# Attention, expert layer and dense layer on one core: the second pair of remainders in four column groups, the dense layer ending with 448 rows, the read in two row tiles

## The chip, the core and the metric

The kernel runs as one launch on one core of a Trainium2 chip. The metric is device time in microseconds of that core. Before the change three runs took 575.08, 575.28 and 576.47 us; the median, 575.28, is the time to compare with.

## What is computed

```python
B, H, S, Ns, D = (4, 8, 512, 32, 64)          # attention
N, D, E, F = (2304, 512, 8, 1024)             # expert layer
n_tokens, d_model, d_ff = (2304, 512, 2048)   # dense layer
...
a = softmax(scale * x @ state.T)              # 512 x 32 per head
xread = a @ state
a2 = softmax(scale * state @ x.T)             # 32 x 512 per head
sread = a2 @ x
rows = concat([xread, sread])                 # 4 * 544 = 2176 rows of 512
...
logits = rows @ w_gate
expert = argmax(logits); gate = softmax(logits)[expert]
disp[e, n] = the n-th row of expert e, while n < capacity
y = relu(disp @ w1[e]) @ w2[e]                # 512 -> 1024 -> 512
out = gate * y[expert, place]                 # zero for rows over capacity
...
h = out @ w_in                                # 512 -> 2048
result = (h * clip(h + 3, 0, 6) / 6) @ w_out  # 2048 -> 512
```

The capacity is 576 rows for each of the 8 experts. In this text layer one is the expert layer and layer two the dense layer.

## The kernel before

**Attention** (`phase1`) goes over the four batches. A batch has eight heads, in two halves f of four heads. `soft_max`, `turn`, `read_max`, `read_exp`, `read_sum` and `read_turn` make the read weights `aT`, 128 partitions (four heads of 32 states) by 128 rows. `read` (line 335) then computes, for block j of 128 rows and half f, one fp32 matmul with K = 128: the stationary operand is `aT`, the moving one is `bd`, a block-diagonal matrix of 264 columns, four heads of 64 values and 8 columns that give the gate's logits. There are 8 reads for each batch, 32 in all; each goes to a PSUM tile `psX` (pool `pX`, three buffers) and is copied to `xrow` by ScalarE (line 344) or, where the table `ALT` says so, by VectorE (line 342). `rows_out` adds the logits of the two halves (line 348) and writes rows of 536 floats to `x_rows` in DRAM.

The order of the instructions of this phase comes from a scheduler: `ln` gives the main steps their order, the tables `AFTER` and `AHEAD` hang side steps to them (`count`, `place`, `lists`, which turn logits into lists of rows by expert, and all of the first expert's tile, named `e_...` and `w..`). `tables` (line 649) then makes small tables on VectorE: `tab` with the expert and rows of each full tile, `tabh` with those of each remainder, `trips` for the loop at the end.

**Layer one.** Up to 256 rows of an expert make a full tile; an expert's remainder of 1 to 64 rows is a half. Six full tiles (NF = 6) and four halves (NQ = 4) are computed in straight code, what is beyond that in a loop at the end. A full tile (`m1`, `m2`) splits weights and rows in two fp32r parts and sums three products. The halves go two by two as a pair (PAIRS: pair 0 beside tile 2, pair 1 beside tile 4), in fp32, the 64 rows of an expert being 64 columns of the array and each expert its own column group:

```python
T.matmul(ps[n][64 * g:64 * g + 64, :],
         th[:, 128 * k + 64 * g:128 * k + 64 * g + 64],
         raws[k, g][:, 512 * n:512 * n + 512], ...)
```

That is line 1070 in `p_m1`. `p_ht` transposes its result (line 1082), `p_m2` (line 1090) is the second layer, `p_y` transposes and writes 128 rows to `y_pad` (line 1099). From here on the order is the order of the code, engine by engine.

**Layer two** works on column tiles of 256 rows: tiles 0 to 5 are the full tiles, tile 6 holds the two pairs. For each of 16 slices m of the 2048 hidden values, `mm3` (line 1115) does twelve fp32r matmuls with 256 moving columns (three products by four blocks of 128), ScalarE and VectorE make the activation and split it in `gh` and `gl` (lines 1127 to 1130), and `mm4` (line 1138) does, for each block t of 128 rows, three matmuls with 512 moving columns into PSUM. `mm4` of a slice is issued behind `mm3` of the next one. Tiles 0 and 1 make the first group, beside which the weights of the layer are converted from 64-bit inputs (`vload`, `vconv`, `prep`); tiles 2 to 6 follow one at a time. `put` (line 1256) scales a block of the result and writes it with an indirect DMA on POOL's queue. In the last tile the second block's `mm4` of the last seven slices (NH) is held back, so that the first block's write is done beside it.

## Time and profile before

| what | value |
|---|---|
| median of three runs | 575.28 us |
| the profiled execution | 573.73 us |
| its span, first to last instruction | 571.5 us |
| PE busy | 550.7 us, 96% |
| DVE busy | 309.8 us, 54% |
| ACT busy | 222.2 us, 39% |
| POOL busy | 142.5 us, 25% |
| mean granted clock of PE | 0.995 |

PE is TensorE, DVE VectorE, ACT ScalarE, POOL GpSimd. The profiled execution took 2.2 us more than its span, which is what lies around the first and the last instruction. A busy engine is not one at its peak: a matmul's record reaches past the start of the next one. An fp32 matmul has two records in the trace, an fp32r matmul one. The attention runs to about 105 us of the span, layer one to 251, the first group of layer two to 343, the last two tiles from 478 to the end.

### The profile page before, as it was taken

What the parts mean: (1) busy time and instruction counts of PE and PEld (TensorE: products, weight loads), DVE (VectorE), ACT (ScalarE), POOL (GpSimd) and SP (SyncE); (2) the same over time, 40 slices, a digit from 0 to 9 for tenths busy, and PEclk for the clock granted to TensorE, in tenths of its full rate; (3) what the DMA queues carried; (4) which work ended last, traced back from release to release, by engine and by line L of the source; (5) the groups of instructions that cost most, each with busy time, mean ns of one, the idle gap of its engine ahead of it and who ended that gap; (6) DMA issues with size and microseconds to landing.
All of it is one profiled execution on the core that took longest, in us unless ns stands there. A gap on an engine that the chain in (4) does not pass through costs nothing.

```text
span 571.5 us, 10466 instructions
## 1 busy us (share of the span) xinstructions
PE 550.7 (96%) x3954; PEld 478.8 (84%) x3954; DVE 309.8 (54%) x700; ACT 222.2 (39%) x462; POOL 142.5 (25%) x195
## 2 busy tenths in 40 slices
PE   6999789999999999999999999999999999999996
PEld 3665589887969696999999889999999999999994
DVE  4888985439625674567778953343333234234331
ACT  4878632235114150424434353333333333333331
POOL 5335734212400110017767732001001001001001
PEclk9999899999999999999999999999999999999999
DMA  6836621997979794235754311001001001000000
GB/s 136 181 122 208 231 103 52 333 377 246 353 260 395 253 342 149 79 124 191 254 204 124 134 39 75 0 24 53 1 18 57 1 18 57 1 1 19 19 2 30
DMA packets 52201, 75.26 MB, mean 132 GB/s; under 512 B 23121, under 2 KB 31313, under 8 KB 51634
## 3 DMA queue, kind: packets, MB, share of 16 engines
q1 hardware_dynamic: 49634, 67.09, 34.9%
q0 software_dynamic: 2240, 7.38, 3.8%
q8 instruction: 33, 0.54, 0.4%
q14 instruction: 22, 0.18, 0.1%
q10 hardware_dynamic: 272, 0.07, 0.1%
HBM read 70.75 MB, written 16.49 MB: 153 GB/s over the span
## 4 chain that ended last, share of the span: by engine, by line
issue 37%; PE 28%; DMA 9%; DVE 5%; ACT 1%; POOL 0%; POOLq 0%; DVEq 0%; ACTq 0%
PE pm L809 10%; PE pm L798 9%; DMA out_dram<-o,fid 6%; PE pm L1090 2%; PE pm L1070 2%; DMA st<-in_moe_w_out_dram 2%; PE p L1115 2%; DVE v L943 2%; DMA st<-in_moe_w_in_dram 1%; DVE v L939 1%; DVE g L1128 1%; DVE v L941 1%; PE po L1138 1%; ACT wh L957 1%; PE pxt L764 1%
## 5 line engine op out<-in xcount | busy, mean ns | idle before, releaser
L1115 PE MATMUL p<-yTh,wh 128*128 128x256 f32 x448 | 110.5, 280 | 0.0
L1115 PE MATMUL p<-yTl,wh 128*128 128x256 f32 x448 | 110.5, 280 | 0.0
L1128 DVE SCALAR_TENSOR_TENSOR g<-u,p 128x256 f32<-128x256 f32 x110 | 46.1, 419 | 115.9 <-ACT u L1127 115.8
L1127 ACT ACTIVATE u<-p,b 128x256 f32<-128x256 f32 x110 | 52.1, 474 | 109.1 <-PE p L1115 109.1
L1115 PEld LDWEIGHTS p<-yTl,wh 128*128 128x128 f32 x448 | 84.4, 188 | 3.9
L1115 PEld LDWEIGHTS p<-yTh,wh 128*128 128x128 f32 x448 | 84.4, 188 | 3.8
L1138 PE MATMUL po<-wh,gh 128*128 128x512 f32 x220 | 86.3, 392 | 0.0
L1138 PE MATMUL po<-wh,gl 128*128 128x512 f32 x220 | 86.2, 392 | 0.0
L1138 PE MATMUL po<-wl,gh 128*128 128x512 f32 x220 | 86.1, 391 | 0.0
L1129 ACT CAST gh<-g 128x256 fp32r<-128x256 f32 x110 | 44.7, 406 | 80.0 <-DVE g L1128 80.0
L1115 PE MATMUL p<-yTh,wl 128*128 128x256 f32 x448 | 71.5, 282 | 0.9 <-POOL wl L958 0.9
L1262 POOL DMA_INDIRECT out_dram<-o,fid x14 | 13.7, 977 | 219.7 <-ACT o L1261 163.6
L1115 PEld LDWEIGHTS p<-yTh,wl 128*128 128x128 f32 x448 | 60.8, 189 | 1.5 <-POOL wl L958 1.5
L1130 DVE TENSOR_TENSOR gl<-g,gh 128x256 fp32r<-128x256 f32 x84 | 36.8, 438 | 39.8 <-ACT gh L1129 39.8
L1138 PEld LDWEIGHTS po<-wh,gl 128*128 128x128 f32 x220 | 41.2, 187 | 9.7 <-POOL gl L1130 0.4
L1138 PEld LDWEIGHTS po<-wh,gh 128*128 128x128 f32 x220 | 41.4, 188 | 5.3
L1138 PEld LDWEIGHTS po<-wl,gh 128*128 128x128 f32 x220 | 41.4, 188 | 5.2
L809 PE MATMUL pm<-hth,w2h 128*128 128x256 f32 x160 | 45.5, 284 | 0.0
L798 PE MATMUL pm<-xth,w1h 128*128 128x256 f32 x160 | 44.6, 283 | 0.7 <-ACT xth L758 0.7
L809 PE MATMUL pm<-hth,w2l 128*128 128x256 f32 x160 | 45.1, 282 | 0.0
L809 PE MATMUL pm<-htl,w2h 128*128 128x256 f32 x160 | 45.0, 282 | 0.0
L958 POOL TENSOR_TENSOR wl<-v,wh 128x1024 fp32r<-128x1024 f32 x14 | 34.8, 2489 | 40.3 <-DMA st<-in_moe_w_in_dram 38.2
(285 smaller groups left out, 1005.1 us busy)
## 6 DMA issues: line engine op xcount, KB each, us to landing
raw<-in_moe_w_dram SPq DMA_DIRECT2D x80, 512.0 KB
st<-in_moe_w_in_dram SPq DMA_DIRECT2D x16, 512.0 KB
st<-in_moe_w_out_dram SPq DMA_DIRECT2D x16, 512.0 KB
x_rows<-xrow SPq DMA_DIRECT2D x4, 1072.0 KB
xb<-in_x_dram SPq DMA_DIRECT2D x32, 128.0 KB
yg<-y_pad SPq DMA_DIRECT2D x14, 258.0 KB
out_dram<-zt SPq DMA_DIRECT2D x2, 1536.0 KB
y_pad<-y SPq DMA_DIRECT2D x5, 516.0 KB
```

The source lines that it names most:

```text
L798: T.matmul(ps[:, j], W1[l][k][:, ls], xT[r][:, k], start=n == 0, stop=n == 11)
L809: T.matmul(ps[:, j], W2[l][k // 2][:, k % 2, ls], hT[k // 2][r][:, k % 2], start=k == 0 and i == 0, stop=k == 7 and i == 2)
L943: V.scalar_tensor_tensor(out=t, in0=lo, scalar=29, in1=t, op0=ALU.logical_shift_right, op1=ALU.bitwise_or)
L958: (V if m in (0, 2) else G).tensor_tensor(out=wl, in0=v, in1=wh.bitcast(F32), op=ALU.subtract)
L1070: T.matmul(ps[n][64 * g:64 * g + 64, :], th[:, 128 * k + 64 * g:128 * k + 64 * g + 64], raws[k, g][:, 512 * n:512 * n + 512], start=i == 0 ...
L1115: T.matmul(pv, l[:, 128 * k:128 * k + 128], r[:, :, 128 * k:128 * k + 128], start=n == 0, stop=n == 11)
L1127: A.activation(out=u, in_=ps, func=AF.Relu, bias=b3)
L1128: V.scalar_tensor_tensor(out=g, in0=u, scalar=6.0, in1=ps, op0=ALU.min, op1=ALU.mult)
L1129: A.copy(gh, g)
L1130: eng.tensor_tensor(out=gl, in0=g, in1=gh.bitcast(F32), op=ALU.subtract)
L1138: T.matmul(po[t], l[:, ls], r[:, 512:1024], start=m == 0 and i == 0, stop=m == 15 and i == 2)
L1262: G.indirect_dma_start(out=out, out_offset=bass.IndirectOffsetOnAxis(ap=fid[:, t:t + 1], axis=0), in_=o, in_offset=None, bounds_check=B * ...
```

## The change

**Layer two** ends with one group of 448 rows in place of the tiles 5 and 6: the 256 rows of tile 5, the 128 of pair 0 and 64 of pair 1. `mm3_j` does the twelve matmuls with 448 moving columns and `act3` twice, for 256 and for 192 columns. `mm4_j` does three matmuls for each of three blocks and two for the last: its 64 rows of `gl` stand beside its 64 rows of `gh` in one stationary operand, and `put(..., half=True)` adds the two halves of the sum. The sums of the last two blocks for the slices after HJ = 12 are held back to the end. **Pair 1** is now for experts whose remainder is at most 32 rows (`halves` sorts the remainders and gives the places): 32 columns of the array for each expert and half of the 1024 hidden values, so four column groups, and in its second layer four groups of 256 moving columns in place of two of 512. **The read** is done with 64 array rows at a time: `bd` has 136 columns (two heads and the logits), and a group of four matmuls fills two PSUM tiles of two blocks each; rows of `x_rows` have 548 floats. `halves` takes over what `tables` did for the remainders, and the copies for the loop (`listed`) are issued later.

```diff
-        ps = pX.tile([128, 264], F32, name="psX", tag="X")
-        T.matmul(ps, s["aT"][:, f, j, :], bd[:, 2 * b + f, :], start=True, stop=True)
...
+        u, a = divmod(i, 2)
+        j0, f = 2 * (u // 2), u % 2
+        if a == 0:
+            s["px"] = [pX.tile([128, 2, 136], F32, name="psX", tag="X") for _ in range(2)]
+            for j in range(2):
+                for r in range(2):
+                    T.matmul(s["px"][r][:, j], s["aT"][64 * r:64 * r + 64, f, j0 + j, :], bd[64 * r:64 * r + 64, 2 * b + f, :], start=True, stop=True)
+        g = PW * (2 * f + a)
+        (V.tensor_copy if f"rd{b}{i}" in ALT else A.copy)(s["xrow"][:, j0:j0 + 2, g:g + 136], s["px"][a])
...
-    for i in (0, 2, 4, 6, 1, 3, 5, 7):
+    for i in range(8):
         ln(read, B - 1, i)
...
-NQ, NHM = 4, 8
+NQ, NHM = 4, 10
...
+NJ = 448
+HJ = 12
...
+    def halves():
+        c, f, te = cnt, Q[0][:, 0, 4:12], Q[3][:, 0, 4:12]
+        q, h = Q[0][:, 1, 4:12], Q[0][:, 2, 4:12]
+        V.tensor_scalar(out=c32, in0=c, scalar1=-32.0, scalar2=None, op0=ALU.add)
+        V.scalar_tensor_tensor(out=q, in0=f, scalar=256.0, in1=c32, op0=ALU.mult, op1=ALU.is_lt)
+        V.scalar_tensor_tensor(out=h, in0=f, scalar=256.0, in1=c, op0=ALU.mult, op1=ALU.is_lt)
...
+    def p_rows(p, g):
+        return [(64 * g, 64)] if p == 0 else [(32 * g, 32), (64 + 32 * g, 32)]
...
-    def p_m1(th, raws):
+    def p_m1(p, th, raws):
+        nb = 2 - p
...
+                    s, w = p_rows(p, g)[n if p else 0]
+                    T.matmul(ps[0 if p else n][s:s + w, :], th[:, 128 * k + s:128 * k + s + w], raws[k, g][:, 512 * n:512 * n + 512],
...
+            for n in range(1 + p):
+                for g in range(2):
+                    if p:
+                        s, m, a = 64 * n + 32 * g, 32, 128 * (k % 4) + 64 * (k // 4) + 32 * g
+                    T.matmul(ps[s:s + m, :], th[:, a:a + m], raws[k // 2, g][:, 512 * (k % 2) + 256 * n:512 * (k % 2) + 256 * n + w],
...
+        if w == 192:
+            gl, tail = gl[:, 0:128], gh[:, 192:256]
+            V.tensor_tensor(out=tail, in0=g[:, 128:192], in1=gh[:, 128:192].bitcast(F32), op=ALU.subtract)
...
+    def mm3_j(m, yTh, yTl):
+        ps = bank3(NJ)
+        sums3(m, ps, *(lambda k, v=v: v[:, k] for v in (yTh, yTl)))
+        return act3(ps[:, 0:256], 256), act3(ps[:, 256:NJ], NJ - 256)
...
+    def mm4_j(m, gg, po, ts):
+        wh, wl = (w[:, 512:1024] for w in WM[m])
+        for t in ts:
+            gh, gl = gg[t // 2]
+            ls = slice(128 * (t % 2), 128 * (t % 2) + 128)
+            ops = ((gh, wh), (gh, wl), (gl, wh)) if t < 3 else ((gh, wh), (gh, wl))
+            for i, (l, r) in enumerate(ops):
+                T.matmul(po[t], l[:, ls], r, start=m == 0 and i == 0, stop=m == 15 and i + 1 == len(ops))
...
-    groups = [(0, 1)] + [(c,) for c in range(2, NCS)]
+    groups = [(0, 1)] + [(c,) for c in range(2, NCS - 2)]
...
+    for m in range(16):
+        gj[m] = mm3_j(m, jh, jl)
+        if m == 0:
+            finish(late)
+            pj = [pM.tile([128, 512], F32, name="po", tag="M") for t in range(4)]
+        else:
+            mm4_j(m - 1, gj[m - 1], pj, (0, 1) if m > HJ else (0, 1, 2, 3))
+    mm4_j(HJ, gj[HJ], pj, (2, 3))
+    for t in range(2):
+        mm4_j(15, gj[15], pj, (t,))
+        put(pj[t], jid[0], t)
+    for t in (3, 2):
+        for m in range(HJ + 1, 16):
+            mm4_j(m, gj[m], pj, (t,))
+        put(pj[t], jid[1], t - 2, t == 3)
```

The order on PE around the last batch's reads (psX is a read's PSUM tile, bank a shared one), before:

```order
L340 MATMUL psX<-bd,aT 128x264
L323 MATMUL bank<-wgs,srT 32x8 x4
L340 MATMUL psX<-bd,aT 128x264 x2
L478 MATMUL bank<-oh,ol 128x144 x2
L340 MATMUL psX<-bd,aT 128x264
L478 MATMUL bank<-oh,ol 128x144
L340 MATMUL psX<-bd,aT 128x264 x3
L798 MATMUL pss<-xT,w1h_91 128x256
L340 MATMUL psX<-bd,aT 128x264
```

With the change the same place on PE reads:

```order
L315 MATMUL bank<-identk,sr 128x128
L344 MATMUL psX<-bd,aT 128x136 x7
L323 MATMUL bank<-wgs,srT 32x8 x4
L344 MATMUL psX<-bd,aT 128x136 x7
L480 MATMUL bank<-oh,ol 128x144 x2
L344 MATMUL psX<-bd,aT 128x136 x2
L835 MATMUL pss<-xT,w1h_93 128x256
```

The 8 reads of 264 columns have become 16 of 136, in three runs that stand closer together; the logits of the state rows (32x8) are now behind seven of them.

The order on PE at pair 1's first layer (raw is a weight block, pth the pair's rows, pm the result), before:

```order
L809 MATMUL pm_2971<-hth_2771,w2h_105 128x256
L809 MATMUL pm_2971<-htl_2772,w2h_105 128x256
L809 MATMUL pm_2971<-hth_2771,w2l_109 128x256
L1070 MATMUL pm_3029<-raw,pth 64x512 x2
L1070 MATMUL pm_3030<-raw,pth 64x512 x2
```

With the change PE has there:

```order
L846 MATMUL pm_3015<-hth_2815,w2h_107 128x256
L846 MATMUL pm_3015<-htl_2816,w2h_107 128x256
L846 MATMUL pm_3015<-hth_2815,w2l_111 128x256
L1135 MATMUL pm_3073<-raw,pth 32x512 x16
L835 MATMUL pm_3108<-xth,w1h_93 128x256
```

Sixteen matmuls that alternate between two PSUM tiles of 64 array columns each are now sixteen into one tile, 32 columns each.

The order on PE in one slice of tile 5 (p is the hidden sum, po the result's sum), before:

```order
L1115 MATMUL p_6797<-yTh_6421,wh_4137 128x256
L1115 MATMUL p_6797<-yTl_6422,wh_4137 128x256
L1115 MATMUL p_6797<-yTh_6421,wl_4138 128x256 x4
L1138 MATMUL po<-wh_4071,gh 128x512
L1138 MATMUL po<-wl_4072,gh 128x512
L1138 MATMUL po<-wh_4071,gl 128x512
L1138 MATMUL po<-wh_4071,gh 128x512
L1138 MATMUL po<-wl_4072,gh 128x512
L1138 MATMUL po<-wh_4071,gl 128x512
```

In one slice of the joined group, with the change, PE has:

```order
L1195 MATMUL p_6257<-yT_5953,wl_3695 128x448 x4
L1242 MATMUL po<-wh_3634,gh 128x512
L1242 MATMUL po<-wl_3635,gh 128x512
L1242 MATMUL po<-wh_3634,gl 128x512
L1242 MATMUL po<-wh_3634,gh 128x512
L1242 MATMUL po<-wl_3635,gh 128x512
L1242 MATMUL po<-wh_3634,gl 128x512
L1242 MATMUL po<-wh_3634,gh 128x512
L1242 MATMUL po<-wl_3635,gh 128x512
L1242 MATMUL po<-wh_3634,gl 128x512
L1242 MATMUL po<-wh_3634,gh 128x512
L1242 MATMUL po<-wl_3635,gh 128x512
```

One slice of one tile had six matmuls of 512 columns behind its twelve of 256; a slice of the joined group has eleven behind its twelve of 448.

## Rows read from the trace of the kernel before

**Rows 1.** The page: PE's busy time, share of the span, instructions.

```profile
PE 550.7 (96%) x3954; PEld 478.8 (84%) x3954; DVE 309.8 (54%) x700; ACT 222.2 (39%) x462; POOL 142.5 (25%) x195
```

**Rows 2.** Busy time by stretch (windows); the first row names the columns.

```profile
core 0: us, PE busy (x) PEld busy (x) DVE busy (x) ACT busy (x) POOL busy (x), PEclk, DMA share, GB/s
...
20.00:40.00 20.00, 19.87 (x199) 12.80 (x198) 16.99 (x46) 15.10 (x39) 6.97 (x10) 1.00 0.50 136
...
60.00:80.00 20.00, 16.33 (x159) 14.01 (x160) 19.37 (x58) 10.62 (x25) 10.18 (x11) 0.91 0.61 222
80.00:104.80 24.80, 23.39 (x191) 22.27 (x190) 15.29 (x80) 6.90 (x17) 10.67 (x20) 1.00 0.29 82
...
189.40:251.30 61.90, 61.90 (x475) 52.15 (x475) 35.17 (x73) 18.75 (x31) 5.07 (x2) 1.00 0.56 192
251.30:342.80 91.50, 90.64 (x587) 81.89 (x586) 71.20 (x101) 40.77 (x82) 57.22 (x39) 1.00 0.47 159
...
478.30:565.90 87.60, 87.57 (x560) 79.10 (x558) 28.91 (x68) 29.46 (x66) 4.86 (x5) 1.00 0.04 15
```

**Rows 3.** Timeline of PE, one tile in layer two: start us, us, operation.

```profile
400.99 0.39 PE L1138 MATMUL po<-wh,gh 128*128 128x512 f32 x1
...
402.35 0.28 PE L1115 MATMUL p<-yTh,wh 128*128 128x256 f32 x1
...
403.76 0.39 PE L1138 MATMUL po<-wh,gh 128*128 128x512 f32 x1
```

**Rows 4.** Timeline of all engines at the end: start us, us, operation.

```profile
565.47 0.40 PE L1138 MATMUL po<-wh,gl 128*128 128x512 f32 x1
...
566.88 0.97 POOL L1262 DMA_INDIRECT out_dram<-o,fid  x1 [2.56 <-DVEq L1361]
```

**Rows 5.** Chain that ended last: start us, us, what.

```profile
189.41 7.02 PE pm L1070 x32
...
208.65 0.87 PE pht L1082 x8
...
221.02 7.02 PE pm L1090 x32
...
231.19 0.44 PE pht L1099 x4
...
251.31 5.57 PE p L1115 x48
```

**Rows 6.** Timeline of PE around line 301 in the attention.

```profile
18.90 0.65 PE L301 MATMUL bank<-xb,e2T 128*32 128x64 f32 x32
19.48 0.66 PE L231 MATMUL psx<-identk,xb 128*128 128x128 f32 x4
```

**Rows 7.** Waits of PE and of DVE, 251 to 343 us: total, times, longest.

```profile
PE p L1115 <- POOL wl L958: 0.9, 2, 0.6
...
DVE g L1128 <- ACT u L1127: 11.6, 9, 2.2
DVE v L939 <- DMA st<-in_moe_w_in_dram: 3.2, 2, 2.5
```

**Rows 8.** Timeline of PE, reads of the attention, second batch.

```profile
38.48 2.47 PE L340 MATMUL psX<-bd,aT 128*128 128x264 f32 x10
```

**Rows 9.** Tile psX: count, duration ns min/median/max, first and last start.

```profile
L340 PE MATMUL psX<-bd,aT x64: 384/386/490, 24.0 to 71.2; 128*128 128x264 f32 x64
L344 ACT COPY xrow<-psX x27: 357/380/419, 24.7 to 71.1; 128x264 f32<-128x264 f32 x27
L342 DVE COPY xrow<-psX x5: 410/419/432, 37.4 to 72.0; 128x264 f32<-128x264 f32 x5
```

**Rows 10.** Timeline of DVE behind the last batch of reads.

```profile
67.45 0.69 DVE L279 STREAM_TRANSPOSE aT<-R 128x512 f32<-128x512 f32 x1
...
72.04 0.42 DVE L342 COPY xrow<-psX 128x264 f32<-128x264 f32 x1
...
72.57 0.19 DVE L348 TENSOR_TENSOR L<-xrow 128x32 f32<-128x32 f32 x1
```

More of the change, by code (lines that the diff above doesn't have):

```diff
@@ L92, in phase1 @@
     st2 = wk.tile([128, 8, 2, D], F32, name="aT")
-    bd = const.tile([128, 8, 264], F32, name="bd")
+    bd = const.tile([128, 8, 136], F32, name="bd")
     sT = const.tile([128, 8, 128], F32, name="sT")
@@ L632, in full @@
     b3 = keep.tile([128, 1], F32, name="b3")
-    Q = [keep.tile([128, 2, 4 + E], F32, name=f"Q{k}") for k in range(4)]
+    Q = [keep.tile([128, 3, 4 + E], F32, name=f"Q{k}") for k in range(4)]
     def consts():
@@ L646, in totals, with scan @@
         T.matmul(ps, onesk, Gf, start=True, stop=True)
+    def scan(a, b):
+        for k, s in enumerate((1, 2, 4)):
+            V.tensor_tensor(out=Q[k + 1][:, a:b, 4:12], in0=Q[k][:, a:b, 4:12], in1=Q[k][:, a:b, 4 - s:12 - s], op=ALU.add)
+    cnt = tb.tile([128, E], F32, name="c")
+    Zt = tb.tile([128, NFM, E], F32, name="Z")
     def tables(ps):
         co = tb.tile([128, E], F32, name="co")
-        c = tb.tile([128, E], F32, name="c")
+        c = cnt
         V.tensor_tensor(out=co, in0=ps, in1=eoffk, op=ALU.subtract)
@@ L886, in full @@
     K = dict(ident=ident, ones=onesk, Gf=Gf, capk=capk, LT=LT, es=es, rote=rote, io8=io8, eoff=eoffk)
-    phase1(tc, x, state, w_gate, capacity, x_rows, K, dict(consts=consts, early=early, zeros=zeros, first=first, tiles=tiles, totals=totals, tables=tables))
+    phase1(tc, x, state, w_gate, capacity, x_rows, K, dict(consts=consts, early=early, zeros=zeros, first=first, tiles=tiles, totals=totals, tables=tables, halves=halves))
     ctx.enter_context(tc.manual_schedule())
@@ L1063, in p_first @@
         pr[p] = p_loads(0, pe[p])
-    def p_m1(th, raws):
-        ps = [pM.tile([128, 512], F32, name="pm1", tag="M") for _ in range(2)]
+    def p_m1(p, th, raws):
+        nb = 2 - p
+        ps = [pM.tile([128, 512], F32, name="pm1", tag="M") for _ in range(nb)]
         for i, k in enumerate((0, 2, 1, 3)):
@@ L1084, in p_ht, with p_m2, p_y @@
         return th
[L1086 to L1087 removed]
+    def p_m2(p, th, raws, gv):
+        w = 512 if p == 0 else 256
+        ps = pM.tile([128, w], F32, name="pm2", tag="M")
         for k in range(8):
[L1089 to L1091 removed]
+            for n in range(1 + p):
[3 more added lines that the diff above has]
+                    else:
+                        s, m, a = 64 * g, 64, 128 * k + 64 * g
+                    T.matmul(ps[s:s + m, :], th[:, a:a + m], raws[k // 2, g][:, 512 * (k % 2) + 256 * n:512 * (k % 2) + 256 * n + w],
+                             start=k == 0, stop=k == 7)
         yr = ew.tile([128, 512], F32, name="pth", bufs=1)
[L1093 removed]
+        A.activation(out=yr[:, 0:w], in_=ps, func=AF.Copy, scale=gv[:, 0:1])
         return yr
[L1096 removed]
+    def p_y(p, yr, idt, row):
+        y = ew.tile([128, 2, YR], F32, name="y", bufs=1)
+        if p:
+            ps = pT.tile([128, 256], F32, name="pht", tag="T")
+            for c in range(2):
+                T.transpose(ps[:, 128 * c:128 * c + 128], yr[:, 128 * c:128 * c + 128], ident)
+            V.tensor_copy(y[:, 0, 0:256].rearrange("p (n c j) -> p n c j", n=2, c=2), ps.rearrange("p (c n j) -> p n c j", c=2, n=2))
+            V.tensor_copy(y[:, 0, 256:260], idt[:, 0:1].broadcast_to([128, 4]))
+            nc.sync.dma_start(out=y_pad[row, 0:260], in_=y[:, 0, 0:260])
+            return
         ps = pT.tile([128, 512], F32, name="pht", tag="T")
@@ L1281, in full @@
                 prep(m + 2)
-            lm, ls, lg, lpo = late
-            for c in ls:
-                if c == NCS - 1 and lm >= 16 - NH:
-                    held[lm] = lg[c]
-                    mm4(lm, *lg[c], lpo[c], (0,))
-                    continue
-                mm4(lm, *lg[c], lpo[c])
-                if lm == 15:
-                    put(lpo[c], ft[c][0][2], 0)
-                    put(lpo[c], ft[c][0][2], 1)
+            finish(late)
             if m == 0:
@@ L1296, in full @@
             late = (m, gs, gg, po)
-            if not last and m >= 10:
-                for c in groups[gi + 1]:
+            if gi + 1 < len(groups):
+                for c in groups[gi + 1] if m >= 10 else ():
                     if m == 10:
```

263 lines of the change are left out of this document (149 added, 114 removed), and 2 rows, old and new, of the table AHEAD.

## The prediction

> **What bounds the kernel now.** I read the shares of the engines first, then the busy time by stretch, then the chain that ended last, then single stretches of the timeline. TensorE (PE) is busy 550.7 of 571.5 us [rows 1]. By stretch [rows 2] PE is full in the rest of layer one (61.90 of 61.90 us between 189.4 and 251.3), nearly full in layer two's first group (90.64 of 91.50) and in the last two column tiles (87.57 of 87.60), all at a granted clock of 1.00, its 2.4 GHz level. Busy time is modelled to the end of a matmul, so I do not price by it: I price by the distance between starts. In the attention PE is full in places (19.87 of 20.00 from 20 to 40 us), but from 60 to 80 us it is VectorE (DVE) that is full, 19.37 of 20.00. So a microsecond taken from PE is worth a microsecond after 105 us, and less than that before.
>
> The profiled execution took 573.73 us, 2.2 us more than its span; the median of the three runs is 575.28, 1.55 above it. I make the sum in the profiled execution's durations and take it off the median.
>
> **Part one, layer two ending with 448 rows.** A tile of 256 rows costs per slice m twelve fp32r matmuls of 256 columns and six of 512. Their starts [rows 3]: 402.35 to 403.76, so 1.41 us for twelve, 117.5 ns each; 400.99 to 402.35, so 1.36 us for six, 227 ns each; 2.77 us in all. Two tiles, each with 16 slices: 32 x 2.77 = 88.6 us. After the change a slice of the joined group has twelve matmuls of 448 columns and eleven of 512 (three for each of three row tiles, two for the tile of 64 rows, whose rounding part rides in the idle half of its stationary operand). No fp32r matmul of 448 columns is in the trace. Its price lies between: as dear as 512 columns (227 ns), or 512's price by columns, 198 ns. I take the straight line between the rows for 256 and 512, 117.5 + 0.75 x 109 = 199 ns, since both neighbours have nearly the same price per column. A slice is then 12 x 0.199 + 11 x 0.227 = 4.89 us, the group 78.2: **minus 10.4 us** (by the dear bound 12 x 0.227 + 2.49 = 5.21 a slice, 83.4, minus 5.2; by the cheap one minus 10.6).
>
> What is beside it: ACT and DVE prepare two pieces per slice, as they did for two tiles. In the last two tiles DVE was busy 28.91 and ACT 29.46 of 87.60 us, so the same work in 78 us stays covered; the extra subtraction of 64 columns is nothing there. The fetch of the four blocks now happens once, in slices 8 to 13 of the tile before, into buffers that nobody reads any more. The sums of the last three slices for the third and fourth block are put behind the others; 9 matmuls of 0.227 then separate the last two writes, so POOL's 0.97 us per indirect write [rows 4] is covered. After the last matmul the same eviction, write and end remain: 565.47 to 571.5, 6.0 us, unchanged.
>
> **Part two, the second pair in four column groups.** Pair one's first layer takes 7.02 us for 32 records, its second also 7.02 [rows 5]. (An fp32 matmul is two records.) These run two at a time, in column groups of 64: one step of two lasts 0.439 us. Now the first layer is 32 records of 512 columns in four groups of 32, the second 64 records of 256 columns. Four at a time gives 8 x 0.439 = 3.51 us for each; two at a time would give 7.02 again, no gain. The trace has four groups of 32 at another place: line 301 starts at 18.90 and the next operation at 19.48 [rows 6], 0.58 us for 32 records of 64 columns. One such record alone lasts 64/512 x 0.439 = 0.055, so 3.0 run at a time with the change of shape counted in, and 8 steps x 0.055 = 0.44 leave 0.14 us for that change. I take four at a time plus 0.14: 3.65 and 3.65, **minus 6.7 us**; at 3.0 at a time it is minus 4.7. Half of the transposes go: four of eight in 0.87 us and two of four in 0.44 [rows 5], **minus 0.65**. All of it is on the chain, which is PE alone there.
>
> What could be late next: the weights. Pair one's second-layer loads wait for its first layer, which now ends 3.4 us sooner, so they start sooner, and a whole layer-one tile of PE work lies between them and their use. After 251.3 the conversion of layer two's weights runs beside PE. PE waited there 0.9 us for a weight part; DVE waited 11.6 us for ACT, that is for PE's results, and only 3.2 us for its own loads [rows 7]. It is mostly paced by PE, so it moves forward with PE.
>
> **Part three, the read in two row tiles.** Before: 32 reads of 264 columns, 64 records; ten of them take 2.47 us [rows 8], from which the last one's tail comes off: (2.47 - 0.386) / 9 = 0.23 us, median duration 386 ns [rows 9]. After: 128 records of 136 columns, 0.23 x 136/264 = 0.12 us each. If the two row tiles run at the same time: 64 x 0.12 = 7.6 us against 14.7; if not, 15.2. No row shows two row tiles, so PE's gain is from minus 7.1 to plus 0.5. The evictions stay: 32 of 272 columns, at 380 ns on ACT and 419 on DVE for 264 [rows 9]. They must now wait for a whole group of four matmuls, and one group holds two of the three PSUM buffers, so the next group waits for the first eviction. Behind the last batch the chain is DVE: the second weight transpose at 67.45, the last eviction at 72.04, the logits' sum at 72.57 [rows 10], about 5 us for evictions that take 8 x 0.4 on two engines. Some of that wait goes, and the queue of a DVE that is full there takes part of it back. I take **minus 1.0 us**; bounds minus 4 and plus 3 (32 changes of array shape at half of 0.14 are 2.2, the buffer waits the rest). The granted clock is 0.91 in this stretch, the only dip; 20 x 0.09 = 1.8 us hang on whether it comes back, inside these bounds.
>
> Here two rules of the Trainium skill speak against the change. "TensorEngine Tiling (Array Packing)", Key Properties, says that a change of tiling mode drains TensorE; the 0.14 us around line 301 [rows 6] agrees in kind, and by it part three alone loses the 2.2 us of the bound. The same page of the Trainium skill, PSUM Bottleneck, says that tiling speeds up TensorE but not the emptying of PSUM; the evictions of 380 and 419 ns [rows 9] against 0.48 us of matmuls for a group of four (8 records, two at a time) bear it out, and by it the reads gain nothing, sum minus 17.8 in place of minus 18.8.
>
> **Edits at nothing.** The tables of the remainders now issue some 13 more small DVE instructions, 0.19 us each [rows 10], 2.5 us before the pairs' weights can be asked for; the pairs come only after another full tile, and PE is busy 23.39 of 24.80 us at that time [rows 2] with the first expert. The wider rows of x_rows (548 for 536 floats) and the shorter last block of y_pad are a few per cent of hidden transfers. Narrower fills of bd and zt at the start are below 1 us and DVE waits for transfers there.
>
> **The sum.** -10.4 - 6.7 - 0.65 - 1.0 = -18.8: profiled 554.9, on the median 575.28 - 18.8 = **556.5 us**.
>
> **Rivals.**
> 1. 448 columns cost as much as 512. For: the price is not proportional below 512 (117.5 ns is more than half of 227). Against: it differs from half by 4 ns only. Part one gives 5.2: 561.7.
> 2. Layer one's gain is swallowed by the conversion of layer two's weights: PE arrives 7 us sooner but the loads and the three DVE steps for each half slice do not follow. For: PE did wait for a weight part, and loads were waited for [rows 7]. Against: the 11.6 us that DVE waited for PE. Then 575.3 - 11.4 = 563.9.
> 3. The read gets slower: the group of four with two of three buffers, and the changes of shape, cost plus 3 in place of minus 1: 560.5.
> 4. Slower: the packing does not hold the remainders. The second pair takes 32 rows of each expert; if a third expert leaves 33 to 64 rows, or a fifth any, a pass of the loop at the end runs, which costs at least one more layer-two tile, 16 x 2.77 = 44 us, and its own layer one: 600.8 or more. It decides from the third such expert. Against: with these inputs the routing, worked out from the reference, gives counts of 512, 512, 576, 64, 32 and 32 rows and two of none; that is six full tiles and remainders of 64 (from the 576), 64, 32 and 32, two and two
>
> **How the numbers follow.** The forecast has 0.74, with a range of its own from 553.0 to 559.5 (part three from -4 to +1, part two from -5.3 to -7.4); rival 1 has 0.09, rival 2 0.08, rival 3 0.07, rival 4 0.02. The range of 8 in 10 goes from 552.5 to 561.9: it holds rivals 1 and 3 and leaves out rivals 2 and 4 and some edges, below 0.2. A measurement of this kernel tells 0.3% (1.7 us) from no change. All but rival 4 are faster by far more, and only a mixture of several rivals with bounds not thought of would end within it: faster 0.97, same 0.01, slower 0.02.
>
> **What would show it.** Right: starts of 448-column matmuls 199 ns apart and slices of 4.9 us; line 1135 and line 1161 of the change 3.6 us each; layer two's first matmul about 8 us sooner (251.31 [rows 5] to 243), its first group as long as before (91.5 us); 6.0 us after the last matmul. Wrong: starts 227 ns apart (rival 1); new PE waits for wl in layer two's first group (rival 2); layer two's first matmul only 4 us sooner with lines 1135 and 1161 as priced (rival 3); instructions in the loop after the last group (rival 4).

## The result, and the profile after

The change makes the kernel about 1% faster, a third of what was forecast: **569.47 us** (median of 4, 568.98 to 570.96) against 575.76 for the kernel before in the same session (575.08 to 576.47). The ratio is 0.9895, interval 0.987 to 0.992; the forecast of 556.5 is 0.967, and 569.47 lies outside its range (552.5 to 561.9). The profiled execution of the changed kernel took 570.96 us, with a span of 569.3 against 571.5. It is the slowest of its four executions, while the profiled one of the kernel before, 573.73, lies below all four in the session: the two profiles are 2.8 us apart where the medians are 6.3 apart, so of a loss that is read from them some 3.5 us can be the spread of executions.

The page, PE's busy time (answers to [rows 1]):

```profile
PE 540.8 (95%) x3836; PEld 471.2 (83%) x3836; DVE 312.2 (55%) x729; ACT 218.0 (38%) x461; POOL 142.8 (25%) x198
```

PE has 9.9 us less work; the span has only 2.2 less. The chain that ended last (start us, us, what; answers to [rows 5]):

```profile
194.21 3.57 PE pm L1135 x32
...
201.03 8.52 PE pm L835 x72
...
210.42 0.44 PE pht L1147 x4
210.86 11.38 PE pm L846 x96
222.24 3.59 PE pm L1161 x64
...
249.21 5.68 PE p L1195 x48
...
553.12 3.25 DMA out_dram<-o,fid
557.14 2.74 DMA out_dram<-o,fid
560.65 2.61 DMA out_dram<-o,fid
564.11 0.89 POOL out_dram L1373
```

The second pair is as forecast: 3.57 and 3.59 us for two times 7.02 [rows 5], and 0.44 for 0.87 of transposes. But layer two's first matmul stands at 249.21, only 2.1 us sooner than 251.31, not 8. And at the end there are three transfers in the chain where one stood before.

Busy time by stretch (columns named in the first row; answers to [rows 2]):

```profile
core 0: us, PE busy (x) PEld busy (x) DVE busy (x) ACT busy (x) POOL busy (x), PEclk, DMA share, GB/s
...
58.00:64.70 6.70, 5.13 (x77) 4.29 (x78) 6.70 (x8) 4.70 (x8) 5.79 (x3) 0.50 0.77 252
64.90:68.10 3.20, 1.36 (x14) 0.93 (x12) 3.20 (x13) 1.04 (x4) 1.35 (x2) 1.00 0.94 308
68.30:78.30 10.00, 10.00 (x51) 9.09 (x52) 7.41 (x30) 5.09 (x14) 4.78 (x6) 0.50 0.45 175
...
60.00:80.00 20.00, 17.42 (x148) 15.40 (x148) 16.56 (x54) 10.41 (x23) 10.12 (x10) 0.62 0.57 202
...
480.90:556.00 75.10, 75.10 (x347) 64.74 (x345) 24.77 (x78) 24.55 (x62) 2.92 (x3) 1.00 0.03 11
```

Between 60 and 80 us the granted clock is 0.62 where it was 0.91 [rows 2]. It is at 0.50, its 1.2 GHz level, in two stretches, 58.0 to 64.8 and 68.2 to 78.4, 17 us in all; in the kernel before it was so for 3.4 us (60.3 to 63.7). PE waits through much of 64.9 to 68.1, and then does ten full microseconds at 0.50: the last reads and the first expert. In the kernel before PE was busier in the same stretch ahead of its last reads, and the clock stayed at 1.00 behind it:

```profile
64.90:68.10 3.20, 2.11 (x17) 1.44 (x15) 2.67 (x13) 2.52 (x7) 2.05 (x3) 1.00 0.96 313
```

The timeline of PE of the changed kernel shows reads of an earlier batch at full clock (the first row), then the waits for DVE's second weight transpose just ahead of the fall, and the last reads at half speed:

```profile
51.88 1.19 PE L344 MATMUL psX<-bd,aT 64*128 64x136 f32 x12
...
66.27 0.73 PE L344 MATMUL psX<-bd,aT 64*128 64x136 f32 x8 [0.74 <-DVE aT L279]
68.19 1.74 PE L344 MATMUL psX<-bd,aT 64*128 64x136 f32 x6 [1.18 <-DVE aT L279]
...
70.38 2.57 PE L344 MATMUL psX<-bd,aT 64*128 64x136 f32 x14
```

The first expert's second layer starts at 89.50 where it started at 86.25 (the changed kernel's row first, then the kernel before's):

```profile
89.50 0.51 PE L846 MATMUL pss<-xb,w2h 128*128 128x256 f32 x2
86.25 0.50 PE L809 MATMUL pss<-xb,w2h 128*128 128x256 f32 x2
```

Layer two's joined group, timeline of PE, one slice (answers to [rows 3]):

```profile
506.20 0.40 PE L1242 MATMUL po<-wh,gh 128*128 128x512 f32 x1
...
508.74 1.79 PE L1195 MATMUL p<-yT,wh 128*128 128x448 f32 x8
...
511.19 0.40 PE L1242 MATMUL po<-wh,gh 128*128 128x512 f32 x1
```

2.54 us for eleven matmuls of 512 columns and 2.45 for twelve of 448, 204 ns each: 4.99 a slice (forecast 4.89). From the first matmul of the last 448 rows to the last matmul it is 474.99 to 555.98, 80.99 us; the two tiles before took 474.74 to 565.47, 90.73. So part one gave 9.7 of its 10.4 us. The end (answers to [rows 4]):

```profile
555.98 0.40 PE L1242 MATMUL po<-wh,gl 128*128 128x512 f32 x1
...
557.14 0.97 POOL L1373 DMA_INDIRECT out_dram<-o,fid  x1 [3.04 <-DMA out_dram<-o,fid]
560.65 0.92 POOL L1373 DMA_INDIRECT out_dram<-o,fid  x1 [2.54 <-DMA out_dram<-o,fid]
564.03 0.97 POOL L1373 DMA_INDIRECT out_dram<-o,fid  x1 [2.46 <-DMA out_dram<-o,fid]
```

From the last matmul's start to the end of the span it is 13.3 us, not 6.0: each write goes out only when the one before has landed, 3.4 to 4.0 us apart, though all four evictions are done by 557.1. The view of POOL's waits (total, times, longest) of the changed kernel:

```profile
POOL out_dram L1373 <- DMA out_dram<-o,fid: 18.8, 7, 3.2
```

The same wait was in the trace of the kernel before, and the prediction did not use it:

```profile
POOL out_dram L1262 <- DMA out_dram<-o,fid: 13.4, 5, 3.2
```

There it cost nothing that shows at the end: the write ahead of the last one had landed at 565.95 (563.34 + 2.61), and the last block was evicted only at 566.60 and written at 566.88 [rows 4].

So two losses are to be explained: some 6 us before layer two by the two profiles (theories C and D below: the read's shape lowers the clock, or something else in the change), and some 7 us at the end (W: the writes wait for one another; P: POOL's issue or the path is that slow).

### The profile page after: what moved, and what is told of

The parts are those of the page before. It is cut to its first block, busy times and chain, and to the rows that moved or that the text cites. A ratio compares the mean times of both kernels' runs of the same rounds, so it can differ in the third digit from the quotient of the medians.

```text
span 569.3 us, 10237 instructions
## 1 busy us (share of the span) xinstructions
PE 540.8 (95%) x3836; PEld 471.2 (83%) x3836; DVE 312.2 (55%) x729; ACT 218.0 (38%) x461; POOL 142.8 (25%) x198
## 3 DMA queue, kind: packets, MB, share of 16 engines
HBM read 70.71 MB, written 16.33 MB: 153 GB/s over the span
## 4 chain that ended last, share of the span: by engine, by line
PE 38%; issue 37%; DVE 10%; DMA 10%; ACT 2%; POOL 1%; SPq 0%; POOLq 0%; DVEq 0%; ACTq 0%
PE pm L835 10%; PE pm L846 10%; DMA out_dram<-o,fid 6%; PE pss L835 2%; DMA st<-in_moe_w_out_dram 2%; PE pm L1161 2%; PE pm L1135 2%; PE pss L846 2%; PE p L1195 2%; PE pss L238 2%; DVE v L1005 2%; PE psX L344 1%; DVE g L1208 1%; DVE v L1001 1%; DMA st<-in_moe_w_in_dram 1%
## 5 line engine op out<-in xcount | busy, mean ns | idle before, releaser
L1195 PE MATMUL p<-yT,wh 128*128 128x256 f32 (+1 forms) x768 | 117.3, 295 | 0.0
L1195 PEld LDWEIGHTS p<-yT,wh 128*128 128x128 f32 x768 | 109.6, 188 | 8.1
L1195 PE MATMUL p<-yT,wl 128*128 128x256 f32 (+1 forms) x384 | 67.3, 297 | 1.2 <-POOL wl L1020 1.2
L1233 PE MATMUL po<-wl,gh 128*128 128x512 f32 x156 | 61.5, 395 | 0.0
L1233 PE MATMUL po<-wh,gh 128*128 128x512 f32 x156 | 61.4, 394 | 0.0
L1233 PE MATMUL po<-wh,gl 128*128 128x512 f32 x156 | 61.4, 394 | 0.0
L1195 PEld LDWEIGHTS p<-yT,wl 128*128 128x128 f32 x384 | 55.5, 189 | 3.0 <-POOL wl L1020 1.8
L835 PE MATMUL pm<-xth,w1l 128*128 128x256 f32 x160 | 44.3, 281 | 0.0
L835 PE MATMUL pm<-xtl,w1h 128*128 128x256 f32 x160 | 42.3, 281 | 0.0
L835 PEld LDWEIGHTS pm<-xth,w1h 128*128 128x128 f32 x160 | 30.1, 188 | 5.7 <-issue 2.1
```

What stands on the lines that cost most here:

```text
L835: T.matmul(ps[:, j], W1[l][k][:, ls], xT[r][:, k], start=n == 0, stop=n == 11)
L1195: T.matmul(out, w[:, 128 * k:128 * k + 128], r(k), start=n == 0, stop=n == 11)
L1233: T.matmul(po[t], l[:, ls], r[:, 512:1024], start=m == 0 and i == 0, stop=m == 15 and i == 2)
```

## The experiments

Medians; the ratio is to the kernel before in the same session.

| run | us | ratio, 95% interval |
|---|---|---|
| changed kernel | 569.47 | 0.9895 (0.987 to 0.992) |
| sums spread | 568.22 | 0.9881 (0.9855 to 0.9908) |
| three writes | 567.11 | 0.9860 (0.9839 to 0.9882) |
| read undone | 569.16 | 0.9886 (0.9864 to 0.9909) |
| kernel before, read alone | 580.99 | 1.0093 (1.0072 to 1.0114) |
| views | 563.44 | 0.9793 (0.9762 to 0.9825) |
| kernel before, views | 574.44 | 0.9997 (0.9975 to 1.0019) |
| kernel before, layout alone | 579.06 | 1.0077 (1.0050 to 1.0104) |
| extra matmuls | 574.54 | 0.9966 (0.9935 to 0.9997) |
| views, addresses restored | 561.80 | 0.9772 (0.9749 to 0.9795) |
| kernel before, layout, restored | 578.27 | 1.0056 (1.0034 to 1.0078) |
| kernel before, read, restored | 580.13 | 1.0089 (1.0066 to 1.0113) |
| views, 64 apart | 561.69 | 0.9778 (0.9754 to 0.9801) |
| views, 192 apart | 562.14 | 0.9776 (0.9757 to 0.9795) |
| kernel before, 192 apart | 573.78 | 0.9980 (0.9964 to 0.9996) |
| views, 192 apart, read undone | 560.13 | 0.9756 (0.9732 to 0.9781) |

### The end: four writes in a row

**Sums spread.**

```
-HJ = 12
+HJ = 9
...
-    mm4_j(HJ, gj[HJ], pj, (2, 3))
-    for t in range(2):
-        mm4_j(15, gj[15], pj, (t,))
-        put(pj[t], jid[0], t)
-    for t in (3, 2):
-        for m in range(HJ + 1, 16):
+    mm4_j(15, gj[15], pj, (0,))
+    put(pj[0], jid[0], 0)
+    for t in (1, 3, 2):
+        for m in range(HJ + 4 if t == 1 else HJ + 1, 16):
...
```

(To hold more pieces, the halves have four and six buffers in place of seven, and the output tiles three in place of four.)

> The changed kernel with another order of its last sums: the joined tile's block 2 and its half block are held back from slice 10 on, not 12, and block 1 from slice 13 on, so that 39 matmuls of 0.23 us, 9.0 us, stand between the end of block 0's sum and the last matmul (18, 4.2 us, in the changed kernel). The same matmuls, evictions and writes. Theory W (each indirect write into the output waits for the one before it to land, 3.5 us from issue to issue, so four in a row need 10.5 us after the first): the first write goes out some 4.8 us sooner against the last matmul, 12.9 us from the last matmul's start to the end become about 8, and the time falls by 5 us, 569.5 to about 564.5. Rival P (the end is long because of the last sums and evictions themselves, or because POOL needs 0.97 us for each write): no more than 1 us gained, 568.5 to 569.5.

Measured 568.22: the direction of W, a quarter of its size. In the trace the first write goes out at 548.46, 4.7 us sooner, as meant, but the second took 4.9 us to land where 2.7 is usual, so the four stand at 548.46, 551.98, 557.61 and 560.99. More room between the sums doesn't help while every write hangs on the landing of another. By the medians alone this run does not decide between W and P.

**Three writes.**

```
-        put(pj[t], jid[1], t - 2, t == 3)
+        if t == 2:
+            put(pj[t], jid[1], t - 2)
```

> The changed kernel with the write of the joined tile's half block left out (its eviction too), so those 64 rows are not written. Theory W (a write waits until the one before it has landed): 3.5 us less, about 566, and three writes stand 3.5 us apart in the tail. Rival P (only POOL's own 0.97 us a write counts): 1 us less, about 568.5.

Measured 567.11, 2.4 us less than the changed kernel's median, between the two; in the trace the three stand at 551.43, 555.33 and 558.86, 3.9 and 3.5 us apart, as W has it, and from the last matmul's start (554.29) to the end of the span it is 9.3 us, 4.0 less than with four.

**Views.** Four views of the output, declared not to overlap, used in turn:

```
...
+    outs = dram_disjoint_views(out, 4)
+    turn_o = [0]
...
-        G.indirect_dma_start(out=out, ...
+        turn_o[0] += 1
+        G.indirect_dma_start(out=outs[turn_o[0] % len(outs)], ...
```

(The kernel before has the same edit.)

> The changed kernel with its writes into the output given in turn to four views of it that are declared not to overlap (each output row is written by one block alone), so that no write has to wait for the one before it; the zeros that are written ahead still come first. Order of the sums, evictions and the writes themselves as in the changed kernel. Theory W (each write waits until the one before has landed, 3.5 us from issue to issue): the last four writes follow their evictions at 553.1, 554.2, 555.7 and 557.1, and the last matmul's start to the end falls from 13.3 us to 6.5: 7 us less, about 562.5. Rival P (POOL's issue and the path of the data take this long anyway): less than 1 us, 568.5 to 569.5.

> The kernel before with the same four views. Theory W: its last write stands at 566.88, 0.3 us after its eviction could be ready, and the write before it 3.5 us ahead, so the wait is hidden there: within 1 us of the kernel before, at most 0.5 us less. If the views bring something by themselves at the earlier writes, all of it shows here: 2 us and more.

Measured 563.44 and 574.44: 6.0 us on the changed kernel, and 0.5 on the kernel before, inside the noise. The timeline at the end of the changed kernel with views:

```profile
552.38 0.97 POOL L1378 DMA_INDIRECT out_dram<-o,fid  x1 [69.94 <-ACT o L1376]
...
553.65 0.97 POOL L1378 DMA_INDIRECT out_dram<-o,fid  x1 [0.30 <-issue]
...
555.17 0.92 POOL L1378 DMA_INDIRECT out_dram<-o,fid  x1 [0.54 <-DVE o L1372]
...
556.59 0.97 POOL L1378 DMA_INDIRECT out_dram<-o,fid  x1 [0.50 <-ACTq L1492]
```

Each write now follows its eviction, and from the last matmul's start (555.24) to the end of the span (561.40) it is 6.2 us where it was 13.3. W is shown: the wait was for a dependency between writes that touch no common row, seen only because all of them name the same tensor. The Trainium skill ("DMA: Bandwidth & Descriptors", Anatomy of one DMA — SWDGE (gpsimd) path) puts a fixed 2.0 us, mostly the write's receipt, on a transfer, plus its bytes at 436 GB/s; for a block of 0.26 MB that is an estimate of 2.6 us. The trace agrees with 2.6 to 2.7 from issue to landing (3.25 for the first of the four); by that estimate most of the chained wait is latency, not traffic.

### Before layer two: the read and its rows

**Read undone.** The changed kernel, one matmul on 128 array rows for each read, and the last batch's reads in the old order (so "the shape" below is the shape with this order):

```
-            for j in range(2):
-                for r in range(2):
-                    T.matmul(s["px"][r][:, j], s["aT"][64 * r:64 * r + 64, f, j0 + j, :], bd[64 * r:64 * r + 64, 2 * b + f, :], ...
...
+        ps = pX.tile([128, 2, 136], F32, name="psX", tag="X")
+        T.matmul(ps, s["aT"][:, f, j, :], bd[:, 2 * b + f, :], start=True, stop=True)
```

> The changed kernel with the attention's read as it was before in its shape on the array: one matmul of 128 array rows and 272 columns with the blocks set apart in bd, in place of four of 64 rows and 136 columns for two of them, in the old order; rows, logits and layout stay as the change has them. Theory C (the read in two row tiles is what lets TensorE's clock drop to 0.5 for 17 us between 58 and 78, where the kernel before has 3.4 us, and costs the 3.2 us by which the first expert's second layer starts later): 566.3, with the clock at 0.5 for about 3 us in 55 to 80. Rival D (the low clock comes from how this execution fell, or from the other parts of the change): the time stays at 569 to 570.5, the read's own gain of about 1 us given back, and a low stretch of 10 us and more stays in 55 to 80 in about as many runs.

**Read alone, on the kernel before**: the change's lines for the read, the rows and the logits, and nothing else of it:

```
-HR = 268
-ROW = 2 * HR
+PW = 137
+ROW = 4 * PW
...
-        T.matmul(ps, s["aT"][:, f, j, :], bd[:, 2 * b + f, :], start=True, stop=True)
+                    T.matmul(s["px"][r][:, j], s["aT"][64 * r:64 * r + 64, f, j0 + j, :], bd[64 * r:64 * r + 64, 2 * b + f, :], ...
...
-        V.tensor_tensor(out=lg, in0=xg[:, 0:n, 256:264], in1=xg[:, 0:n, HR + 256:HR + 264], op=ALU.add)
+        V.tensor_reduce(out=lg, in_=xg[:, 0:n].rearrange("p n (g c) -> p n c g", g=4)[:, :, 128:136], ...
```

> The kernel before with the change's read alone: two tiles of 64 array rows, the row layout of four groups of 137, the logits summed from four parts, the rows written and fetched so; pairs, tables and layer two as before. Theory C (two row tiles bring the low clock): about 3 us slower than the kernel before, 578 to 579. Rival D: within 1 us of the kernel before, and faster by up to 1 us if the forecast's term holds (574.7).

Measured 569.16 and 580.99. The two contradict each other: on the kernel before the read costs 5.3 us, by more than theory C had, and undoing its shape in the changed kernel brings 0.3. So what costs cannot be the shape alone; the row layout, which "read undone" keeps, had to be split off. The traces show in part where the gain of "read undone" went. In its profiled execution the clock is at 0.50 for 10.2 us, not 17, and layer one's first full tile starts 1.5 us sooner (103.24 for 104.77); but its matmuls then wait, 0.41 us at 135.2 and 1.81 at 140.3 where the changed kernel waits 0.80, and both are at the same place again. The changed kernel, then "read undone":

```profile
140.35 0.39 PE L835 MATMUL pm<-xth,w1h 128*128 128x256 f32 x1 [0.80 <-DVE y L850]
140.28 0.39 PE L832 MATMUL pm<-xth,w1h 128*128 128x256 f32 x1 [1.81 <-DVE y L847]
```


**Layout alone, on the kernel before**: the same, with the matmul of the read as in "read undone".

> The kernel before with the change's row layout alone (four groups of 137 columns, logits summed from four parts) and the read left as one matmul of 128 array rows and 272 columns in the old order: the same kernel as the one with the read alone but for the read's shape on the array. Theory C (the shape, two row tiles of 64, brings the low clock and the 5.3 us that the read alone cost): within 1 us of the kernel before, clock at 0.5 for about 3 us between 55 and 80. Rival L (longer rows, other reductions and the order that the scheduler makes of them bring it): 4 to 5 us slower than the kernel before, as with the read alone, 580.

Measured 579.06, 4.1 us slower than the kernel before in its session: theory C falls as the main cause. The shape adds 1.2 to it (5.3 for 4.1, each against the kernel before in its own session). The windows of the stretch 55 to 80 us, read alone, layout alone and the kernel before:

```profile
55.00:80.00 25.00, 19.86 (x164) 17.19 (x162) 21.53 (x59) 13.77 (x30) 14.67 (x13) 0.66 0.58 201
```

```profile
55.00:80.00 25.00, 17.92 (x166) 14.88 (x164) 24.87 (x70) 14.39 (x31) 16.66 (x14) 0.86 0.59 202
```

```profile
55.00:80.00 25.00, 18.73 (x174) 15.79 (x174) 24.18 (x70) 13.93 (x31) 14.86 (x14) 0.93 0.57 200
```

The shape goes with a lower clock, 0.66 for 0.86; but the layout costs its 4.1 us with the clock nearly as before, 0.86 for 0.93.

**Extra matmuls** in the changed kernel, where PE waits:

```
+            for r in range(2 if b == B - 1 else 0):
+                T.matmul(s["px"][r], sT[:, 0, :], bd[:, 0:2, :], start=True, stop=True)
```

> The changed kernel with eight extra matmuls of 272 columns (constants times constants, overwritten by the read that follows), two ahead of each group of the last batch's read, 0.37 us each, 3 us of TensorE in all, where TensorE waits. If the clock is what costs (TensorE's waits between 55 and 69 let it fall, and the half clock then doubles the reads and the first expert), the clock stays at 1.0 for more of 55 to 80, layer two of the first expert starts 1 to 3 us sooner than 89.5, and the time falls by 1 to 2 us. If it is the order and the waits for DVE and ACT themselves, the extra work adds 0 to 2 us: 569.5 to 571.5.

Measured 574.54, slower than either forecast. In the profiled execution the clock did not stay up: it was 0.66 in 60 to 85 us, where the changed kernel has 0.70, and the first expert's second layer starts at 95.82, not before 89.50. So that PE's waits let the clock fall is not borne out by this run; it stays an argument. Its executions show how time and clock go together, though: 568.5 us at a mean granted clock of 0.988, 576.1 to 577.0 at 0.975 to 0.977. Nothing here shows how to hold it.

**What the layout does to layer one's matmuls.** The chain's last tile of layer one in the kernel before, and with the layout alone (L798 is its first matmul, L809 its second; 72 and 96 records):

```profile
231.63 8.18 PE pm L798 x72
239.81 11.50 PE pm L809 x96
```

```profile
234.19 8.52 PE pm L798 x72
242.71 11.39 PE pm L809 x96
```

The same instructions on the same shapes: 8.18 / 72 is 113.6 ns before, 8.52 / 72 is 118.3 (118.2 by the starts alone) after; the second matmul has 119.8 and 118.6. In every kernel with the longer rows and no pads, the changed one too (8.52 and 11.38 above), these pitches hold in tiles 2 to 5. What differs is where the tiles lie in SBUF: of a partition the gathered token tile takes 4384 bytes for 4288, and the zero tile ahead of everything 2192 for 3136, so all that lies behind them moves.

Layer two's matmuls change as well. From its first output write to the last matmul, the start of the one to the start of the other, the kernel before takes 222.40 us (343.07 to 565.47), and so it does in its runs with views and 192 apart; with the layout alone it takes 223.92 (346.14 to 570.06), and so with the read alone. Of the 4.6 us between the spans of the two profiles, 571.5 and 576.1, 1.3 stand before layer one's first full tile (100.93 for 102.26), and 3.3 behind it, where the instructions of PE are the same: 1.5 up to layer two, 0.3 in its first group, 1.5 in the rest. The next four runs each differ from the run they are compared with in the pads alone.

**Addresses restored** modulo 128 (shown for the changed kernel with views; on the kernel before the first pad is of 8 floats):

```
+    pad = keep.tile([128, 16], F32, name="pad")
...
-        xg = ew.tile([128, 2, ROW], F32, name="xg", bufs=3)
+        xg = ew.tile([128, 2 * ROW + 8], F32, name="xg", bufs=3)[:, 0:2 * ROW].rearrange("p (t c) -> p t c", t=2)
```

> The changed kernel with the four views, and with two pads alone (64 bytes ahead of the zero tile, 32 bytes behind each gathered token tile) that put the weights, the turned tokens and the hidden tiles of layer one, and the weights and sums of layer two, at the same SBUF address modulo 128 as in the kernel before; not one instruction differs from the kernel with the views but for its addresses. Theory A (a matmul's pitch hangs on how its two operands lie against each other: 113.6 ns against 118.2 ns for layer one's first matmul with the longer rows): that pitch is 113.6 to 114.0 again in tiles 1 to 5, layer two's matmuls lose 0.7 and 2.5 ns, and the time falls by 2 to 4 us against the views alone: 559.5 to 561.5. Rival O (the pitch comes from what the other engines do at the time, in the order that the scheduler made): same time within 1 us, 563, pitch 118.

> The kernel before with the row layout alone, as in the run with the layout alone (4.1 us slower than the kernel before), and two pads (32 bytes ahead of the zero tile, 32 bytes behind each gathered token tile) that put the operands at the kernel before's addresses modulo 128. Theory A: 3 to 4 us of the 4.1 come back, 575 to 576. Rival O: 578.5 to 579.5 as without the pads.

> The kernel before with the read alone (layout and two row tiles), and the same two pads. Theory A with theory C for the rest (the two row tiles let the clock fall for longer, 2 us): 577 to 578, with layer one's pitch at 113.6 in tiles 2 to 5 and a mean granted clock of about 0.982. If the read in two row tiles is worth the 1 us of the forecast once the addresses are as before: 574.

**64 bytes apart**: the token tile's 8 floats without the first pad, and

```
+                fit.append(ew.tile([128, 24], F32, name="padh", bufs=1))
             hT.append([ew.tile([128, 2, 256], F32R, name=f"ht{h}{q}", bufs=1) for h in "hl"])
...
+            fit.append(mw.tile([128, 16], F32, name="padw", bufs=1))
...
+        fit.append(mw.tile([128, 16], F32, name="pady", bufs=1))
         t = mw.tile([128, 2, 2, DM], F32R, name="yT2", bufs=1)
+        fit.append(mw.tile([128, 16], F32, name="padz", bufs=1))
```

> The changed kernel with the four views and pads chosen so that the two operands lie 64 bytes apart modulo 128 everywhere: layer one's weights and turned tokens, its second weights and the hidden tiles, layer two's weights and all three sums' inputs, and the activated halves and the output weights. Theory A, with the rule that the traces so far bear out (64 apart: 113.6 ns; the same: 118.6; 32 apart: 118.2 to 119.9): layer one's pitch 113.6 in both of its matmuls, layer two's first matmul of 256 columns 116 to 117, and 1 to 5 us less than with the addresses of the kernel before: 556 to 560. Rival O: 563.

Measured 561.80, 578.27, 580.13 and 561.69. All pitches move, though no instruction does, so the placement does set them; but to 117.8 and 118.3 ns (restored) and 117.8 and 117.8 (64 apart), not to 113.6. The rule modulo 128 falls. The gains are 1.6 and 1.8 us on the views, 0.8 on the layout alone; these compare different sessions, and the intervals overlap, so the medians alone do not tell them from noise. The traces do: on the layout alone the pads take 0.5 us off layer one (151.2 for 151.7) and 0.7 off the stretch of 223.92, which is 223.22 in both of these padded runs on the kernel before. That is 1.2 of the 3.3. The read's shape costs 1.9 us with these pads (580.13 for 578.27, one session).

Laid side by side, the pitches went by the distance in bytes from weights to moving tile modulo 512, which is worked out from the tiles' addresses in the programs (a trace does not show it): 192 gave 113.6, 64 gave 117.8, 480 gave 118.2, 384 gave 118.6, 96 gave 119.9, for the first matmul and the second alike. One tile spoke against it from the start: tile 1 of the kernel before, at the same 192, has 117.8.

**192 bytes apart** in both matmuls:

```
-            xT_pad.append(ew.tile([128, 16], F32, name="pad", bufs=1))
+            xT_pad.append(ew.tile([128, 72], F32, name="pad", bufs=1))
         xT = [ew.tile([128, 4, 256], F32R, name=f"xt{h}", bufs=1) for h in "hl"]
+        if len(xT_pad) == 1:
+            xT_pad.extend(ew.tile([128, 2, 256], F32R, name=f"ht{h}{q}", bufs=1) for q in range(4) for h in "hl")
```

(On the kernel before only the last two lines.)

> The changed kernel with the four views, the pad ahead of the turned tokens widened by 224 bytes, and the hidden tiles placed right behind the turned tokens, so that weights and moving operand lie 192 bytes apart modulo 512 in both matmuls of layer one. No instruction is added or moved. Theory A512 (the pitch goes by that distance): 113.6 ns in place of 118.2 and 118.6 in tiles 1 to 5, 4.5 us of TensorE less, and 3 to 4.5 us less than with the views alone: 559 to 560.5. Rival O (the order and the other engines set the pitch): 118 ns again, 563.

> The kernel before with its hidden tiles placed right behind the turned tokens, so that layer one's second matmul too has 192 bytes between its operands modulo 512 (96 before); nothing else differs. Theory A512: its pitch falls from 119.9 ns to 113.6, 3.0 us of TensorE over tiles 1 to 5, and the time by 2 to 3 us, 572 to 573. Rival O: no change, 575.

Measured 562.14 and 573.78. The kernel before with it, the chain's last tile:

```profile
231.04 8.18 PE pm L798 x72
239.22 10.91 PE pm L809 x96
```

The second matmul falls from 119.9 to 113.6 ns in some tiles (10.91 / 96) and to 117.8 in others, and the first rises to 117.8 in one; in the changed kernel it is alike. So where the tiles lie sets the pitch in part: 113.6 was seen at 192 alone, but 192 gave 117.8 as well, and what decides between the two from tile to tile stays open. On the changed kernel 1.3 us came of the 3 to 4.5 forecast (563.44 to 562.14), on the kernel before 1.4 of 2 to 3 (575.22 to 573.78).

**192 apart, and the read undone as well.**

> The changed kernel with the four views, with 192 bytes between the operands as in the run above, and the read on 128 array rows as before the change. Theory A512 with theory C (the two row tiles let TensorE's clock fall for longer, which cost 1.9 us both with and without the pads on the kernel before): 0 to 2 us less than the run above, 558 to 560, mean granted clock 0.987 and more. If the read's shape is worth the forecast's 1 us: 1 us more than the run above.

Measured 560.13, 2.0 us less than with the read in two row tiles (the two intervals overlap), clock 0.988 for 0.981 in the profiled executions. This is the fastest version run: 15.1 us below the kernel before in its session and 9.3 below the changed kernel's median. It keeps the packing, the 448 rows and the row layout, and drops the row tiles.

## Why the prediction was wrong

By its own steps:

1. *Layer two with 448 rows, minus 10.4.* Right: 9.7. The straight line for 448 columns was 5 ns short (204 for 199), the 512-column pitch 4 (231 for 227); the tiles that went had cost 90.7, not 88.6. Rival 1 is out: 227 was its price.
2. *The second pair, minus 6.7 and minus 0.65.* Right: 6.9 (14.04 to 7.16), and half of the transposes went.
3. *The read, minus 1.0, bounds minus 4 and plus 3, and "the wider rows of x_rows" at nothing.* This step failed, beyond its bound: alone it costs 5.3 us. The step took over PE's time of the reads, and there its range held: twelve of them take 1.19 us at full clock (51.88 in the timeline of PE above); less the last one's 0.276 they stand 83 ns apart, 10.6 us for 128 records against 14.7. But what it left at nothing, the wider rows, costs 4.1, and the row tiles 1.2 more; two other pairs of runs have 1.9 and 2.0 for the row tiles, and in the changed kernel itself undoing them brought only 0.3. All four go with the lower clock. The sentence that 1.8 us hang on whether the clock comes back saw the place and counted only on a gain: the clock is at 0.50 for 17 us in place of 3.4. That PE falls because it has less to do between its waits is argued, not shown, and the extra matmuls speak against it. The Trainium skill ("TensorE: Matmul & The Clock Gate", Part 1: The HAM clock gate) says that the clock is held at half when TensorE has been idle; the rows agree in part, 1.36 us busy of 3.20 ahead of the second fall: TensorE was waiting for more than half of that time, not for all of it. Rival 3 was the right place with too small a price.
4. *"POOL's 0.97 us per indirect write is covered"*, and *6.0 us after the last matmul, unchanged.* This step failed too: 13.3. The step priced the issue of a write and not what the next write waits for. It is the term that was missing, 6.0 us by the run with views.
5. *The conversion moves forward with PE.* Nearly: from layer two's first matmul to its first output write it took 93.2 us (249.21 to 342.44) against 91.8 (251.31 to 343.07). Part of that is layer two's pitch (5.68 us for its first 48 matmuls against 5.57 [rows 5]); rival 2 as it was put, 7 us swallowed, is out.

The sum with what was measured: -9.7 - 7.5 + 5.3 + 6.0 = -5.9, against -6.3. So most of the error sits in steps 3 and 4 (that their prices add up like this is itself not shown, with 0.3 for the read undone), and each was a side effect of an edit that was priced by its own instructions.

Of the layout's cost, 3.3 of the 4.6 us in its profile stand behind the attention, where PE's instructions are unchanged and their pitch is not; pads alone took 1.2 of that back, and the rule of the pitch stays open. The other 1.3 are lost in the attention (1.2 of it before 88 us), where the scheduler orders the same work another way; which of the differences counts there was not tried.

## What to carry to other kernels

Ask of every transfer at the end not how long its issue takes but what the next one waits for: a view of who waits for the output tensor would have shown 13.4 us of waits, hidden until the work between the writes was taken away. A change of a tile's size moves every tile behind it, and matmuls that the change never touches can alter their pitch by 4%; compare the pitch of untouched matmuls first. And work taken from TensorE in a stretch where it waits for others is not sure to be a gain: look at the granted clock beside the busy time, since here the time went with the clock.

## What was not expected of the hardware

- The pitch of one and the same fp32r matmul (128x256, weights loaded for each) was 113.6, 117.8, 118.2, 118.6 or 119.9 ns at a granted clock of 1.00, and pads that only moved its operands in SBUF changed it; 192 bytes apart modulo 512 gave both the lowest and 117.8.
- A block of 128 rows by 2 KB takes 2.7 us from issue to landing, but one in the spread run took 4.9 for no reason that the profile shows.
- The fp32r matmul of 448 columns takes 204 ns where the line between 256 and 512 gave 199: the price stays nearly proportional there.
- The stretch with fewer TensorE instructions kept it busy for longer: 17.42 us of 60 to 80 with 148 records against 16.33 with 159 [rows 2], at a granted clock of 0.62 against 0.91.
